# Loading the first chunks in pairs, with the first weight slices among them

## The chip, the cores and the metric

The kernel runs on one core of a Trainium2 chip. The metric is the device time of one launch in microseconds (us); lower is better. The time is 1.7 to 2.2 us longer than the span of the trace, which runs from the first to the last instruction.

The engines are called as in the profile: PE is TensorE (the matmuls), PEld its weight loads, DVE is VectorE, ACT is ScalarE, POOL is GpSimd, and SP is the engine that issues the data moves. "L565" is a line of the kernel.

## The reference, cut to what matters

```python
B, H, S, D = 4, 8, 768, 64              # q, k, v: float32
for t in range(S):                       # attention with a decaying state
    state = gamma[h] * state + outer(k[:, :, t], v[:, :, t])
    y[:, :, t] = (q[:, :, t] @ state) / sqrt(D)
x = y.transpose(0, 2, 1, 3).reshape(B * S, H * D)      # 3072 x 512
h = maximum(x @ w_in, 0.0)                             # 512 -> 2048
out = (h * h) @ w_out                                  # 2048 -> 512
```

A token's 64 numbers of one head lie together in memory, 256 bytes, and the next token of the same head follows. Two tokens of one head are therefore 512 bytes in one piece.

## The kernel before: the parts that matter

The 3072 tokens are 24 chunks of 128. For each chunk, q, k and v are loaded, cast to bf16, q and k are transposed ("turned") by PE or by the data queue, and a "visit" of PE computes scores, values and the state. DVE writes the result, scaled, to the tile `xt`. Then the first feed-forward matmuls (F1, L565) multiply `xt` by `w_in`, and the second ones (F2, L608) by `w_out`. F1 works on blocks of one to four chunks, and an F1 matmul has as many columns as the block has tokens.

```python
BLOCKS = [1, 1, 1, 1, 1, 1, 2, 2, 2, 4, 4, 4]     # chunks per F1 block
ORDER = (                                          # loads: i = slice of w_in, o = slice of w_out
    "k0 q0 q1 v0 k1 q2 v1 k2 v2 v3 k3 q3 i0 i1 q4 o0 i2 i3 k4 o1 v4 o2 o3 v5 v6 q5 k5 q6 v7 q7 k6 k7")
# ... (cut)
ld = {x: sb(f"{x}n", [P, NLD, H * D], FP32) for x in "qkv"}       # load tiles, after smaller tables
# ... (cut)
def prepare(m):                                    # one chunk: rows of 64 floats, 256 bytes
    for x in "kqv":
        t = ld[x][:, slot, :]
        # issued by SP (cut)
        q_.dma_start(t.rearrange("s (h d) -> s h d", h=H),
                     src[x][b, :, i * C : (i + 1) * C, :].rearrange("h s d -> s h d"))
    # ... casts of k and q on any of DVE, ACT, POOL; v times a table on DVE (cut)
# ... F2 of the last chunk is made in two half rows; prio decides their order (cut)
prio=(q4 + F2LAG) * 8 + 2 * j + 1 + part * 0.5
```

The order on each engine is not written by hand. A planner, run at build time, lays every operation in time by a model of the engines, the loads and the instruction fetches, and emits the instructions in that order. The planner also puts filler matmuls on PE while it waits at the start.

## Time and profile before

| | before |
|---|---|
| median of 3 runs | 216.29 us (215.98 to 216.98) |
| span of the profiled run | 214.5 us |
| first F1 matmul starts | 21.93 us |
| PE full and at full clock from | 26.3 us |
| last matmul ends | 210.4 us |

First the page of the profiled run: the span in 40 equal slices of 5.4 us. A digit is the busy share in tenths, PEclk is the granted clock of PE in tenths, and GB/s is what the data engines moved.

```profile
span 214.5 us, 6317 instructions
...
PE   6664899999999999999999999999999999999992
...
PEclk9965599999999999999999999999999999999999
...
GB/s 144 219 220 320 351 346 352 344 225 257 224 222 174 193 209 205 193 179 206 212 243 213 165 219 210 208 212 185 155 58 52 3 71 27 3 49 49 33 112 53
```

PE is full from the sixth slice to the end, so it bounds the kernel from there. The first five slices are different: PE is 40 to 90% busy, its clock falls to a half, and the loads move only about 220 GB/s in slices 2 and 3, against about 350 later. The same in the windows view; the columns are named by its first line, and the last two are the share of the 16 data engines and GB/s. The share adds up the times of all packets, and it is above 1 in places (1.34 at 5 to 11 us).

```profile
core 0: us, PE busy (x) PEld busy (x) DVE busy (x) ACT busy (x) POOL busy (x), PEclk, DMA share, GB/s
5.00:11.00 6.00, 4.20 (x80) 2.21 (x78) 2.99 (x6) 1.90 (x3) 2.45 (x4) 1.00 1.34 220
18.00:26.30 8.30, 6.84 (x136) 5.75 (x136) 5.55 (x12) 3.54 (x6) 2.73 (x4) 0.50 1.08 369
26.30:210.50 184.20, 183.37 (x2448) 108.83 (x2440) 100.68 (x205) 76.26 (x129) 30.78 (x47) 1.00 0.80 170
```

What PE waits for at first is in the chain of work that ended last, in order of time (start, duration, what):

```profile
13.32 7.64 DMA wst<-in_moe_w_in_dram
...
21.01 0.88 POOL w_in L345
...
21.93 3.59 PE fps L565 x32
```

Twelve loads of q, k and v are issued one behind the other until 13.3 us. Only then is the first slice of `w_in` issued, which takes 7.64 us to land and 0.88 to cast. The first 32 F1 matmuls then run at half clock.

The issue list gives the median time from issue to landing, and the waits of the data queue show what the end of the program waits for (total, times, longest, in us). The last view is of the loads and stores in the stretch from 210.5 to 214.5 us, in 40 slices of 0.1 us.

```profile
kn<-in_k_dram SPq DMA_DIRECT2D x24, 256.0 KB, 5.5
...
wst<-in_moe_w_in_dram SPq DMA_DIRECT2D x4, 1024.0 KB, 9.8
```

```profile
SPq L686 <- DMA out_dram<-osb: 2.1, 1, 2.1
```

### The profile page before, as it was taken

The numbers are of one execution on the slowest core, as the hardware profiler recorded it, in microseconds if no ns is written. First come the engines' busy times: TensorE is split into PE (matmuls) and PEld (weight loads), VectorE is DVE, ScalarE is ACT, GpSimd is POOL, SyncE is SP. The second block draws the span as 40 slices with busy tenths as digits, with TensorE's granted clock in tenths as the row PEclk, the third lists the DMA queues.
The fourth block names the chain that finished last, engine by engine and source line by source line (L and its number), as shares of the span: only waits on it lengthen the run. The fifth ranks groups of instructions, "written<-read, shape, count | busy, mean of one in ns | idle before, by whom it ended". The sixth has DMA issues, their size and how long they took to land.

```text
span 214.5 us, 6317 instructions
## 1 busy us (share of the span) xinstructions
PE 200.8 (94%) x2764; PEld 119.8 (56%) x2764; DVE 115.4 (54%) x249; ACT 87.5 (41%) x145; POOL 39.9 (19%) x68
## 2 busy tenths in 40 slices
PE   6664899999999999999999999999999999999992
PEld 2343899675467787666654444454444444444461
DVE  1567778775148699666745674656654433322100
ACT  8223368643234264433321644223534325534211
POOL 5413322314321222122231213132100000000000
PEclk9965599999999999999999999999999999999999
DMA  7999999999999999989999999999811010011021
GB/s 144 219 220 320 351 346 352 344 225 257 224 222 174 193 209 205 193 179 206 212 243 213 165 219 210 208 212 185 155 58 52 3 71 27 3 49 49 33 112 53
DMA packets 99627, 38.15 MB, mean 178 GB/s; under 512 B 92304, under 2 KB 92560, under 8 KB 99600
## 3 DMA queue, kind: packets, MB, share of 16 engines
q1 hardware_dynamic: 99600, 37.76, 81.8%
q8 instruction: 21, 0.34, 0.7%
q14 instruction: 6, 0.05, 0.1%
HBM read 27.26 MB, written 6.29 MB: 156 GB/s over the span
## 4 chain that ended last, share of the span: by engine, by line
PE 83%; DMA 6%; SPq 6%; ACT 1%; issue 1%; POOL 0%; DVE 0%; ACTq 0%
PE fps L608 38%; PE fps L565 38%; SPq L355 6%; DMA wst<-in_moe_w_in_dram 4%; DMA qkT<-kqs 3%; PE yy L425 2%; PE yy L440 2%; PE sc L451 1%; PE sc L462 1%; ACT qkT L387 0%; PE fps L408 0%; POOL w_in L345 0%; ACT osb L616 0%; PE yy L381 0%; DVE xt L527 0%
## 5 line engine op out<-in xcount | busy, mean ns | idle before, releaser
L565 PE MATMUL fps<-xt,w_in 128*128 128x128 bf16 (+2 forms) x768 | 94.0, 276 | 0.7 <-POOL w_in L345 0.6
L608 PE MATMUL fps<-w_out,h 128*128 128x512 bf16 (+1 forms) x400 | 92.2, 371 | 0.0
L570 ACT ACTIVATE h<-fps 128x512 bf16<-128x512 f32 x96 | 57.3, 597 | 75.2 <-PE fps L565 75.2
L565 PEld LDWEIGHTS <-w_in 128*128 128x128 bf16 x768 | 60.6, 100 | 29.1 <-POOL w_in L345 0.8
L575 DVE TENSOR_TENSOR h<-h 128x512 bf16<-128x512 bf16 x96 | 44.2, 469 | 48.3 <-ACT h L570 48.1
L608 PEld LDWEIGHTS <-h 128*128 128x128 bf16 x400 | 37.5, 98 | 36.8
L616 ACT ACTIVATE osb<-fps 128x512 f32<-128x512 f32 (+1 forms) x25 | 14.5, 580 | 31.5 <-PE fps L608 30.4
L345 POOL CAST kqs<-kn 128x512 bf16<-128x512 f32 x24 | 15.9, 664 | 56.3 <-DMA kn<-in_k_dram 46.8
L527 DVE TENSOR_TENSOR xt<-yy,yf 128x512 bf16<-128x512 f32 x24 | 16.5, 687 | 16.2 <-PE yy L440 13.3
L345 POOL CAST kqs<-qn 128x512 bf16<-128x512 f32 x24 | 15.7, 654 | 37.5 <-DMA qn<-in_q_dram 37.5
L366 DVE TENSOR_TENSOR vs<-vn,vf 128x512 bf16<-128x512 f32 x24 | 17.7, 740 | 7.2 <-DMA vn<-in_v_dram 7.2
L505 DVE TENSOR_TENSOR pt<-sc,cmask 128x512 bf16<-128x512 f32 x24 | 16.3, 680 | 4.8 <-PE sc L462 4.8
L518 DVE TENSOR_TENSOR state<-sc,state 128x256 bf16<-128x256 f32 x40 | 16.7, 418 | 0.7
L440 PE MATMUL yy<-qkT,state 64*64 64x64 bf16 x352 | 12.3, 203 | 0.5
L408 PE MATMUL fps<-ident,kqs 128*128 128x128 bf16 x48 | 5.6, 249 | 4.6 <-POOL kqs L345 4.6
L425 PEld LDWEIGHTS <-vs 64*64 64x64 bf16 x384 | 5.3, 112 | 7.6 <-issue 7.4
L462 PE MATMUL sc<-vs,kqs 64*64 64x64 bf16 x352 | 7.9, 198 | 1.1 <-DVE vs L366 1.1
L451 PE MATMUL sc<-qkT 64*64 64x64 bf16 x384 | 7.7, 198 | 1.2 <-ACT qkT L341 0.7
L440 PEld LDWEIGHTS <-state 64*64 64x64 bf16 x352 | 7.7, 112 | 1.2 <-PE yy L440 1.2
L341 ACT ACTIVATE qkT<-fps 128x512 bf16<-128x512 bf16 x6 | 3.6, 597 | 11.3 <-PE fps L408 11.3
L408 PEld LDWEIGHTS <-kqs 128*128 128x128 bf16 x48 | 3.4, 108 | 8.2 <-POOL kqs L345 7.7
L425 PE MATMUL yy<-pt,vs 64*64 64x64 bf16 x384 | 8.0, 203 | 0.0
(32 smaller groups left out, 53.5 us busy)
## 6 DMA issues: line engine op xcount, KB each, us to landing
kn<-in_k_dram SPq DMA_DIRECT2D x24, 256.0 KB, 5.5
qn<-in_q_dram SPq DMA_DIRECT2D x24, 256.0 KB, 5.3
vn<-in_v_dram SPq DMA_DIRECT2D x24, 256.0 KB, 5.2
out_dram<-osb SPq DMA_DIRECT2D x23, 256.0 KB, 2.8
wst<-in_moe_w_in_dram SPq DMA_DIRECT2D x4, 1024.0 KB, 9.8
wst<-in_moe_w_out_dram SPq DMA_DIRECT2D x4, 1024.0 KB, 10.6
qkT<-kqs SPq DMA_TRANSPOSE x16, 4.6
out_dram<-osb SPq DMA_DIRECT2D x2, 128.0 KB, 2.2
```

What stands on the lines that cost most here:

```text
L345: nc.gpsimd.tensor_copy(o, t)
L366: lambda: nc.vector.tensor_tensor(out=o[:], in0=t.rearrange("s (h d) -> s h d", h=H), in1=vf[:, i, :, None].to_broadcast([P, H, D]), op=AL ...
L425: nc.tensor.matmul(yy[L * c : L * c + L, sub, p * L : p * L + L], lhsT=vs[r, 4 * a + j, :], rhs=pt[r, a, j, :], start=(p == 0), stop=True, ...
L440: nc.tensor.matmul(yy[L * c : L * c + L, sub, p * L : p * L + L], lhsT=st[r, j, :], rhs=qkT[r, 1, j, sub * L : sub * L + L], start=False, ...
L505: lambda: nc.vector.tensor_tensor(out=pt[:], in0=sc[:, :, 0:256].rearrange("s g (p t) -> s g p t", p=NJ), in1=cmask[:, None, None, :].to_b ...
L518: f = lambda cc=cc, j1=j1, j0=j0: nc.vector.tensor_tensor(out=sts[j1][:], in0=cc, in1=sts[j0][:], op=ALU.add)
L527: lambda: nc.vector.tensor_tensor(out=xt[:, :, u * C : u * C + C].rearrange("s p (g t) -> s g p t", g=2), in0=yy[:, :, 0:256].rearrange("s ...
L565: nc.tensor.matmul(ps[:, u * n : u * n + n], lhsT=w_in_bf[j][:, cb, c * P : (c + 1) * P], rhs=xt[:, cb, cols], start=(cb == 0), stop=(cb = ...
L570: nc.scalar.activation(h2[:, f0 : f0 + per, cols], ps[:].rearrange("p (u n) -> p u n", u=per), AF.Relu)
L575: nc.vector.tensor_mul(hv, hv, hv)
L608: nc.tensor.matmul(ps[:, 0:w], lhsT=h2[:, fb, u * C : u * C + C], rhs=w_out_bf[j][:, c, ns], start=(fb == 0), stop=(fb == NFB - 1))
L616: lambda o1=o1, slot=slot, ns=ns, w=w: nc.scalar.activation(osbs[slot][:, ns], fps[o1["op"]["bank_index"]][:, 0:w], AF.Copy),
```

## The change

Its intent is to bring the first weights earlier by making the early loads faster. Chunks 0 and 1, and chunks 2 and 3, are loaded as pairs: row s of the tile holds tokens 2s and 2s+1, so that each piece is 512 bytes. The tokens are then in the wrong rows. For k and v, PE puts them in order by matmuls with a 0/1 matrix ("placing"), and ACT copies the result out of the accumulator. For q and k, even and odd tokens are turned apart and written interleaved. The first slice of `w_in` goes between the pairs. Chunks 8 and 9, which the data queue turned, are turned by PE. Block sizes begin with 2. Forty tiny matmuls of one column stand at the head of PE's program. The last two half rows are made one after the other. The planner's model got finer constants too.

```diff
-BLOCKS = [1, 1, 1, 1, 1, 1, 2, 2, 2, 4, 4, 4]
+BLOCKS = [2, 1, 1, 1, 1, 2, 4, 2, 2, 4, 4]
-WARM = 20.0
-FILL = 0.8
-PACE = 8
+WARM = 14.0
+FILL = 0.215
+WARMING = 5.5
+PACE = 6
-NPE = 6
-NTD = 8
+NPE = 7
+NTD = 10
+PRE = 40
+NPAIR = 2
... (planner constants and engines for casts cut)
 ORDER = (
-    "k0 q0 q1 v0 k1 q2 v1 k2 v2 v3 k3 q3 i0 i1 q4 o0 i2 i3 k4 o1 v4 o2 o3 v5 v6 q5 k5 q6 v7 q7 k6 k7"
+    "k0 v0 q0 k2 v2 i0 q2 i1 q4 i2 o0 o1 k4 i3 k5 v4 q5 o2 q6 v5 v6 o3 q7 k6 k7 v7"
 )
... (cut)
+    def together(n):
+        b, i = where(2 * n)
... (cut)
+                   lambda x=x: nc.sync.dma_start(
+                       rows_(x).rearrange("s (h n) -> s h n", h=H),
+                       src[x][b, :, i * C : (i + 2) * C, :].rearrange("h (s g) d -> s h (g d)", g=2)),
... (casts, turning of even and odd tokens cut)
+                    for g in range(2):
+                        nc.tensor.matmul(ps[:], lhsT=perm[r, g, :], rhs=twin[name][r, g, :], start=(g == 0), stop=(g == 1))
... (cut)
-                                prio=(q4 + F2LAG) * 8 + 2 * j + 1 + part * 0.5, lat=0.2,
+                                prio=(q4 + F2LAG) * 8 + 2 * j + 1 + part * 9, lat=0.2,
... (cut)
+            one = nc.const_aps.tensor(1.0, [P, 1], BF16)
+            for _ in range(PRE):
+                nc.tensor.matmul(fps[NBANK - 1][0:1, 0:1], lhsT=one, rhs=one, start=True, stop=True)
```

More of the change, by code (lines that the diff above doesn't have):

```diff
@@ L26 @@
     DMA_LATENCY = 1.9
+    GEN_LATENCY = 1.65
     LAND = 1.25
@@ L82, in schedule @@
                     pool[e].add(o["i"])
-        bank_free = [0.0] * (nbanks - 1) + [WARM]
+        if "PE" in eng_free:
+            eng_free["PE"] = 0.06 * PRE
+        bank_free = [0.0] * (nbanks - 1) + [WARM + 1]
         bank_of = {}
         open_groups = set()
-        pipe = 0.0
+        pipe = made = 0.0
+        late = []
         outstanding = {e: [] for e in eng_free}
         done = 0
-        issued, edge, next_fetched, history, crossed = 0, self.BLOCK0, 3.0, [], 0.0
+        issued, edge, next_fetched, history, crossed = 2 * PRE, self.BLOCK0, 3.0, [], 0.0
         while done < n:
@@ L116, in schedule @@
             if move:
-                cost, n_desc, hold = dur
+                gen, cost, n_desc, hold = dur
                 out_ = outstanding[eng]
@@ L132, in schedule @@
                 eng_free[eng] = t + hold
-                pipe = max(pipe, t + self.DMA_LATENCY) + cost
-                end[i] = pipe + self.LAND
-                out_.append((pipe, n_desc))
+                if n_desc:
+                    made = max(made, t + self.GEN_LATENCY) + gen
+                    ready = made + 0.15
+                else:
+                    ready = t + hold + 0.5
+                pipe = max(max(pipe, t + self.DMA_LATENCY) + cost, ready)
+                late = [y for y in (max(max(y, t + self.DMA_LATENCY) + cost, ready) for y in late) if y > pipe + 0.05]
+                end[i] = max([pipe] + late) + self.LAND
+                out_.append((max([pipe] + late), n_desc))
                 dur = hold
@@ L139, in schedule @@
                     o["fill"] = 0
-                    if t < WARM:
-                        o["fill"] = int(max(0.0, t - max(eng_free[eng], 1.5) - 0.3) * FILL / 0.427)
+                    if WARM - WARMING < t < WARM + 1:
+                        o["fill"] = int(max(0.0, t - max(eng_free[eng], WARM - WARMING) - 0.1) / FILL)
                     issued += 2 * o["fill"]
+                    before = issued
                     todo, per = 2 * o["count"], dur / max(1, 2 * o["count"])
@@ L156, in schedule @@
                     history.append((issued, t + dur))
+                    if any(before < x <= issued for x in range(self.BLOCK0 - self.AHEAD, issued + 1, self.BLOCK)):
+                        late.append(max(pipe, t + 0.4) + 1.27)
                     o["dur"] = dur
@@ L174, in schedule @@
         return sorted(range(n), key=lambda i: (start[i], i))
-SMALL = (1.20, 65, 0.6)
-TURN = (1.10, 16, 2.4)
-WIDE = (2.85, 33, 0.6)
-STORE = (0.80, 9, 0.6)
-BLOCKS = [1, 1, 1, 1, 1, 1, 2, 2, 2, 4, 4, 4]
+SMALL = (1.20, 0.93, 65, 0.6)
+TWIN = (1.20, 1.75, 65, 0.6)
+TURN = (0.60, 1.10, 16, 2.4)
+WIDE = (0.60, 2.80, 33, 0.6)
+STORE = (0.30, 0.80, 9, 0.6)
+BLOCKS = [2, 1, 1, 1, 1, 2, 4, 2, 2, 4, 4]
 SPLIT = 6
 AHEAD = 4
-WARM = 20.0
-FILL = 0.8
-PACE = 8
+WARM = 14.0
+FILL = 0.215
+WARMING = 5.5
+PACE = 6
 LEAD = 2
-NPE = 6
-NTD = 8
-QACT = 0
+NPE = 7
+NTD = 10
+PRE = 40
+CVT = {'DVE': 0.69, 'POOL': 1.1}
+TCAST = {'DVE': 0.43, 'ACT': 0.63, 'POOL': 0.78}
+TEVAC = {'ACT': 0.6, 'DVE': 0.62}
+MEVAC = {'ACT': 0.6}
+NPAIR = 2
 F2LAG = 3.0
@@ L244 @@
         assert 512 % (n * C) == 0 and x // 4 == (x + n - 1) // 4
-    NLD, NBF, NQT, NXT, NH2, NWS, NOSB, NST = 4, 5, 5, 4, 3, 4, 3, 6
+    NLD, NBF, NQT, NXT, NH2, NWS, NOSB, NST = 4, 6, 6, 4, 3, 4, 3, 6
     NBANK = 4
@@ L260 @@
     vf = sb("vf", [P, NCH, H], FP32)
-    pos_i = sb("pos_i", [P, S], I32)
     yf = sb("yf", [P, NJ, S], FP32)
@@ L266 @@
     bf["v"] = [sb(f"vs{j}", [P, H, D], BF16) for j in range(NBF)]
-    qkts = [sb(f"qkT{j}", [P, 2, NJ, P], BF16) for j in range(NQT)]
+    qkt_all = sb("qkT", [P, NQT, 2, NJ, P], BF16)
+    qkts = [qkt_all[:, j] for j in range(NQT)]
+    perm = sb("perm", [P, 2, P], BF16)
+    ex2_i = sb("ex2_i", [P, NCH // 2, 2], I32)
+    ex2_f = sb("ex2_f", [P, NCH // 2, 2, H], FP32)
+    vf2 = sb("vf2", [P, NCH // 2, 2, H], FP32)
     pts = [sb(f"pt{j}", [P, 2, NJ, L], BF16) for j in range(2)]
@@ L271 @@
     h2s = [sb(f"h2{j}", [P, NFB, 512], BF16) for j in range(NH2)]
+    twins = [{x: h2s[NH2 - 1][:, 6 * j + 2 * "qkv".index(x) : 6 * j + 2 * "qkv".index(x) + 2, :] for x in "qkv"}
+             for j in range(2)]
+    pos_i = h2s[NH2 - 1][:, 12:15, :].rearrange("p a n -> p (a n)").bitcast(I32)
     w_in_bf = [sb(f"w_in{j}", [P, NCB, 512], BF16) for j in range(4)]
@@ L315, in halflogs, with placing @@
                 nc.vector.memset(lnt[L * c : L * c + L, p : p + 1], float(np.log(gammas[4 * a + 2 * b + c])))
+    def placing():
+        nc.gpsimd.memset(perm[:], 0.0)
+        for half in range(2):
+            r = slice(L * half, L * half + L)
+            nc.gpsimd.affine_select(out=perm[r], in_=perm[r], compare_op=ALU.not_equal,
+                                    fill=1.0, base=0, pattern=[[-1, 2], [1, P]], channel_multiplier=-2)
     pl.add("iota", "POOL", 0.2, (), ("ex_i",),
@@ L322 @@
     pl.add("cmask", "POOL", 0.9, (), ("cmask",), mask, prio=-96)
+    pl.add("perm", "POOL", 1.2, (), ("perm",), placing, prio=-95.5)
+    pl.add("iota3", "POOL", 0.2, (), ("ex2_i",),
+           lambda: nc.gpsimd.iota(ex2_i[:], pattern=[[2 * C, NCH // 2], [1, 2]], base=0, channel_multiplier=2), prio=-98.5)
     pl.add("lng", "DVE", 0.4, (), ("lng",), logs, prio=-99)
@@ L332 @@
            lambda: nc.vector.tensor_scalar_mul(vf[:], vf[:], scale), prio=-99)
+    pl.add("ex2_f", "DVE", 0.2, ("ex2_i", "lng"), ("ex2_f",),
+           lambda: nc.vector.tensor_tensor(
+               out=ex2_f[:], in0=ex2_i[:, :, :, None].to_broadcast([P, NCH // 2, 2, H]),
+               in1=lng[:, None, None, :].to_broadcast([P, NCH // 2, 2, H]), op=ALU.mult), prio=-99)
+    pl.add("vf20", "ACT", 0.3, ("ex2_f",), ("vf2",),
+           lambda: nc.scalar.activation(vf2[:], ex2_f[:], AF.Exp, scale=-1.0), prio=-99.5)
+    pl.add("vf2", "DVE", 0.2, ("vf2",), ("vf2",),
+           lambda: nc.vector.tensor_scalar_mul(vf2[:], vf2[:], scale), prio=-99)
     def ytable():
@@ L336, in ytable @@
             nc.scalar.activation(yf[:, p, :], pos_i[:], AF.Exp, scale=lnt[:, p : p + 1])
-    pl.add("yf", "ACT", 3.4, ("pos_i", "lnt"), ("yf",), ytable, prio=-98)
+    yf_made = pl.add("yf", "ACT", 3.4, ("pos_i", "lnt"), ("yf",), ytable, prio=-98)
     def copy_on(eng, o, t):
@@ L345, in copy_on, with turn_fn, place @@
             nc.gpsimd.tensor_copy(o, t)
+    twin_users = [yf_made]
+    def together(n):
+        b, i = where(2 * n)
+        m, s0, w, twin = 2 * n, (2 * n) % NLD, n % 2, twins[n % 2]
+        rows_ = lambda x: ld[x][:, s0 : s0 + 2, :].rearrange("s u n -> s (u n)")
+        held = lambda x: (f"ld{x}{s0}", f"ld{x}{s0 + 1}")
+        for x in "kqv":
+            pl.add(f"ld{x}{m}", "SP", TWIN, (), held(x),
+                   lambda x=x: nc.sync.dma_start(
+                       rows_(x).rearrange("s (h n) -> s h n", h=H),
+                       src[x][b, :, i * C : (i + 2) * C, :].rearrange("h (s g) d -> s h (g d)", g=2)),
+                   prio=dma_prio[(x, m)])
+        for g in range(2):
+            for x in "kq":
+                o = twin[x][:, g, :].rearrange("s (j a d) -> s a j d", a=2, j=NJ)
+                t = rows_(x).rearrange("s (a j g d) -> s a j g d", a=2, j=NJ, g=2)[:, :, :, g, :]
+                pl.add(f"c{x}{m}.{g}", TCAST, 0, held(x), (f"twin{x}{w}.{g}",),
+                       lambda on, t=t, o=o: copy_on(on, o, t), prio=urgency(m))
+            t = rows_("v").rearrange("s (h g d) -> s h g d", h=H, g=2)[:, :, g, :]
+            pl.add(f"cv{m}.{g}", CVT, 0, held("v") + ("vf2",), (f"twinv{w}.{g}",),
+                   lambda on, t=t, g=g: (nc.vector if on == "DVE" else nc.gpsimd).tensor_tensor(
+                       out=twin["v"][:, g, :].rearrange("s (h d) -> s h d", h=H), in0=t,
+                       in1=vf2[:, i // 2, g, :, None].to_broadcast([P, H, D]), op=ALU.mult),
+                   prio=urgency(m))
+        q0 = m % NQT
+        for g in range(2):
+            for x, name in enumerate("kq"):
+                o1 = {}
+                def turn_fn(x=x, name=name, g=g, o1=o1):
+                    ps = fps[o1["op"]["bank_index"]].bitcast(BF16)
+                    for j in range(NJ):
+                        nc.tensor.transpose(ps[:, j * P : j * P + P], twin[name][:, g, j * P : j * P + P], ident[:])
+                i0 = pl.add(f"T{name}{m}.{g}", "PE", 0.26, (f"twin{name}{w}.{g}", "ident"), (f"gT{name}{m}{g}",), turn_fn,
+                            prio=-200 + m, lat=0.2, count=4, bank=("open", ("T", m, x, g), False))
+                twin_users.append(i0)
+                o1["op"] = pl.ops[i0]
+                pl.add(f"E{name}{m}.{g}", TEVAC, 0, (f"gT{name}{m}{g}",),
+                       (f"qkT{q0}.{name}{g}", f"qkT{q0 + 1}.{name}{g}"),
+                       lambda on, x=x, g=g, o1=o1: copy_on(
+                           on, qkt_all[:, q0 : q0 + 2, x].rearrange("p c j (t g) -> p c j t g", g=2)[:, :, :, :, g],
+                           fps[o1["op"]["bank_index"]].bitcast(BF16)[:, 0:512].rearrange("p (j c t) -> p c j t", j=NJ, c=2)),
+                       prio=urgency(m), lat=0.05, bank=("close", ("T", m, x, g)))
+        for c in range(2):
+            r = slice(L * c, L * c + L)
+            for name in "kv":
+                o1 = {}
+                def place(name=name, r=r, o1=o1):
+                    ps = fps[o1["op"]["bank_index"]]
+                    for g in range(2):
+                        nc.tensor.matmul(ps[:], lhsT=perm[r, g, :], rhs=twin[name][r, g, :], start=(g == 0), stop=(g == 1))
+                i0 = pl.add(f"N{name}{m + c}", "PE", 0.45, (f"twin{name}{w}.0", f"twin{name}{w}.1", "perm"), (f"gN{name}{m + c}",),
+                            place, prio=-190 + m + c, lat=0.2, count=2, bank=("open", ("N", m + c, name), False))
+                twin_users.append(i0)
+                o1["op"] = pl.ops[i0]
+                o = bf[name][(m + c) % NBF]
+                o = o.rearrange("s j a d -> s (j a d)") if name == "k" else o.rearrange("s h d -> s (h d)")
+                pl.add(f"M{name}{m + c}", MEVAC, 0, (f"gN{name}{m + c}",), (f"bf{name}{(m + c) % NBF}",),
+                       lambda on, o=o, o1=o1: copy_on(on, o, fps[o1["op"]["bank_index"]][:]),
+                       prio=urgency(m + c), lat=0.05, bank=("close", ("N", m + c, name)))
@@ L348, in prepare @@
     def prepare(m):
+        if m < 2 * NPAIR:
+            if m % 2 == 0:
+                together(m // 2)
+            return
         b, i = where(m)
@@ L352, in prepare @@
             t = ld[x][:, slot, :]
-            side = x == "q" and m < QACT
-            pl.add(f"ld{x}{m}", "ACT" if side else "SP", SMALL, (), (f"ld{x}{slot}",),
-                   lambda x=x, t=t, q_=nc.scalar if side else nc.sync: q_.dma_start(
+            pl.add(f"ld{x}{m}", "SP", SMALL, (), (f"ld{x}{slot}",),
+                   lambda x=x, t=t: nc.sync.dma_start(
                        t.rearrange("s (h d) -> s h d", h=H),
                        src[x][b, :, i * C : (i + 1) * C, :].rearrange("h s d -> s h d")),
-                   prio=dma_prio[(x, m)] - 200 * side)
+                   prio=dma_prio[(x, m)])
         for x in "kq":
@@ L371, in qkeys @@
     def qkeys(m):
-        return [f"qkT{m % NQT}.{x}" for x in "kq"]
+        return [f"qkT{m % NQT}.{x}{g}" for x in "kq" for g in range(2)]
     def flips(m):
@@ L394, in transpose @@
         qkT, t = qkts[m % NQT], kq[m % NBF]
-        if NPE <= m < NTD:
+        if m < 2 * NPAIR or NPE <= m < NTD:
             return
@@ L411, in transpose @@
             o1["op"] = pl.ops[i0]
-            pl.add(f"E{name}{m}", EVAC, 0, (f"gT{name}{m}",), (qkeys(m)[x],),
+            pl.add(f"E{name}{m}", EVAC, 0, (f"gT{name}{m}",), qkeys(m)[2 * x : 2 * x + 2],
                    lambda on, x=x, o1=o1: copy_on(on, qkT[:, x].rearrange("p j t -> p (j t)"),
@@ L582, in ffn1 @@
             pl.add(f"R{blk}.{f0}", "ACT", 0.6, (f"g{grp}",), hk, relu,
-                   prio=blk0[blk] + f0 / 16 * nb, bank=("close", grp))
+                   prio=blk0[blk] + f0 / 16 * nb, bank=("close", grp),
+                   after=twin_users if g == NH2 - 1 else ())
             pl.add(f"Q{blk}.{f0}", "DVE", 0.43, hk, hk, square, prio=blk0[blk] + f0 / 16 * nb + 2)
@@ L656 @@
                 for _ in range(o.get("fill", 0)):
-                    nc.tensor.matmul(fps[NBANK - 1][:], lhsT=ident[:],
-                                     rhs=ident[:, None, :].to_broadcast([P, 4, P]), start=True, stop=True)
+                    nc.tensor.matmul(fps[NBANK - 1][:, 0 : 2 * P], lhsT=ident[:],
+                                     rhs=ident[:, None, :].to_broadcast([P, 2, P]), start=True, stop=True)
                 o["fn"](o["on"]) if o["flex"] else o["fn"]()
```

## The prediction

> **What bounds it now.** The windows view shows TensorE (PE) busy 183.35 of the 184.18 us between 26.32 and 210.5 us, at full granted clock. PE binds from there on. The start is bound by loads: in the chain of waits the load queue issues until 13.3 us, the first w_in slice takes 7.64 us to land, its cast 0.9, and the first FFN matmul starts at 21.93. The granted clock is 0.50 from about 13 to 26 us, so the first 32 FFN matmuls take 3.59 us instead of 1.79.
>
> **Why the load is slow.** In the windows of 1 us the twelve q, k, v loads before the weights move 214 to 230 GB/s (4.5 to 16 us; nearly all packets under 512 B), the weight loads after them 390 to 414. [...] Pairing makes the rows 512 B. My estimate is about 300 GB/s, 1.75 us for 512 KB against 2.4 for two loads now.
>
> **Change, step by step.**
> - Removed: the first w_in slice now follows five pair loads (about 9 us of data, estimate) instead of twelve single ones (14.4). It should land near 14.5 to 15.5, and the first FFN matmul start at about 15.7: 6.2 us earlier.
> - Added, mostly in PE time that waits anyway: eight placing groups (two 512-column matmuls each, about 0.43 to 0.85 us), their ACT evacuations (0.6 each). Two more chunks turned by PE instead of the DMA queue cost about 0.9 us net in the saturated part.
> - Block sizes are neutral: 16 FFN matmuls of 128 columns take 0.89, 8 of 256 columns 0.87.
> - Not regained: after the change only two chunks are ready at the first slice (1.8 us of work), and the second slice lands about 4.5 us after the first, since a pair load lies between. I expect 1.5 to 2 us idle at about 17.5 to 20 us, and perhaps a second cold phase[...] (warm at 6 to 12.5 us, cold after 12.5 at 40 to 75% busy).
> - Tail: the last two half-row groups one after the other instead of interleaved hide one 0.38 us evacuation.
> - The 40 tiny matmuls lie before any data: worth nothing by themselves.
>
> **Sum.** Work left at 26.32 us before: 183.3. For a start at 15.7 add first FFN group 1.8, visits 2 and 3 about 2, late turns 0.6, extra turns 0.75: 188.4. Plus 2 idle, 0.9 of scattered gaps, 0.5 to 1 of cold clock: last matmul at about 207.7 instead of 210.4. With the tail, about 3.2 us of 216.3 saved.
>
> **Predicted: 213.0 us**, 8 in 10 between 209.8 and 215.8. Chances: faster by over 2% 0.31, within 2% 0.64, slower 0.05.
>
> **What would show it.** GB/s in the first 11 us near 300, not 220; first FFN matmul at 15 to 16.5; a PE gap and perhaps a clock of 0.5 at 17 to 22; PE full from 25 us.
>
> **What would make it wrong.** Pair loads at 350 GB/s or more and a warm clock throughout (209 to 211). Or ACT, which alone evacuates the placed rows, delaying the first visits; the fourth w_in slice, moved behind two w_out slices, starving PE near 30 us; the early four-chunk block waiting for chunk 11 near 80 us (then 215 or more).

The 300 GB/s is the author's estimate; it lies between the two rates measured in the trace of the kernel before (214 to 230 and 390 to 414), and how the rate goes with the length of the rows had not been shown. The 0.5 to 1 us of cold clock is an estimate too, after the clock of 0.50 in the same trace.

## More of the kernel before

The kernel before had a median of 216.41 us in the batch of the first comparison and 215.77, 215.73 and 216.12 us in the three batches of experiments.

```profile
GB/s 0 0 0 0 0 0 0 10 236 338 358 266 113 215 348 317 266 72 82 0 0 0 31 20 20 10 0 0 0 0 0 0 0 0 0 0 0 0 0 0
...
q14 instruction: 1, 0.01, 0.6%
```

The last stores are nearly done at 212.4 us, but a few packets trail at 10 to 31 GB/s until 213.1, and an instruction fetch lies in the same stretch. The program waits 2.1 us for this.

## The result, and the profile after

| | before | after |
|---|---|---|
| median, 4 runs each | 216.41 us (215.98 to 216.98) | 213.19 us (212.94 to 213.53) |
| ratio | 1 | 0.9851, 95% interval 0.9821 to 0.988 |
| span of the profiled run | 214.5 us | 211.8 us |
| first F1 matmul starts | 21.93 us | 19.51 us |
| PE full and at full clock from | 26.3 us | 21.35 us |
| last matmul ends | 210.4 us | 208.65 us |
| from there to the end of the span | 4.1 us | 3.1 us |

A ratio is the mean time of one kernel's fast runs over that of the other's fast runs of the same rounds, so it is not quite the ratio of the medians quoted. The kernel is 1.5% faster, inside the band of 2% that counts as the same. A second batch, given below as a control, measured 213.76 us and 0.9922, so there the kernel gained 0.8%.

The page of the kernel after:

```profile
span 211.8 us, 6380 instructions
...
PE   2898999999999999999999999999999999999994
...
PEclk9999999999999999999999999999999999999999
...
GB/s 167 290 344 343 348 352 239 302 300 183 268 217 210 184 219 190 258 206 233 173 238 211 203 227 220 237 165 76 0 53 50 3 50 50 3 51 50 0 102 99
```

GB/s in the second slice went from 219 to 290. PE is 80% busy or more from the second slice, but much of that is placing and filler. The clock row now reads 9 from the start, and here it misleads. The trace records changes of the clock, and the first recorded one is at 21.36 us; before it the row shows full clock because nothing was recorded. The instructions tell otherwise. The F1 matmuls at 19.51 us need 1.91 us for eight of 256 columns; at 21.73 us the trace has sixteen in 1.92 us. PE ran at half speed until about 21.36 us. That was not fixed by the program: t2 below has the same instructions up to its end, and its trace has full clock from 11.6 to 18.4 us (a mean of 0.94 over the first 26.32 us).

The windows view of the kernel after, with the same columns as before:

```profile
5.00:11.00 6.00, 4.87 (x27) 2.32 (x28) 3.06 (x6) 3.97 (x8) 3.81 (x4) 1.00 1.21 290
...
21.35:208.70 187.35, 186.62 (x2569) 111.00 (x2568) 103.78 (x216) 79.11 (x134) 31.44 (x47) 1.00 0.80 168
```

The second line accounts for PE's gain. PE is saturated 4.95 us earlier (26.3 less 21.35), but it has 3.25 us more left to do (186.62 less 183.37), and its gaps in the stretch fell from 0.83 to 0.73. That is 4.95 - 3.25 + 0.1 = 1.8 us, and the last matmul ends 210.41 - 208.65 = 1.8 us earlier.

The timeline around the first slice of `w_in` (start, duration, engine, and in brackets the idle time before and who ended it) shows why F1 does not start right after it:

```profile
14.92 0.61 POOL L392 CAST w_in<-wst 128x512 bf16<-128x512 f32 x1 [0.70 <-DMA wst<-in_moe_w_in_dram]
...
16.68 0.42 DVE L390 CAST w_in<-wst 128x512 bf16<-128x512 f32 x1
...
18.00 0.63 ACT L388 ACTIVATE h<-qn 128x512 bf16<-128x512 f32 x1 [0.54 <-DMA qn<-in_q_dram]
...
18.24 0.69 DVE L642 TENSOR_TENSOR xt<-yy,yf 128x512 bf16<-128x512 f32 x1 [0.35 <-PE yy L555]
...
18.68 1.03 PE L430 MATMUL fps<-ident,h 128*128 128x128 bf16 x8 [0.50 <-ACT h L388]
19.51 0.63 PE L680 MATMUL fps<-xt,w_in 128*128 128x256 bf16 x2
```

The slice has landed at 14.9 us and its last quarter is cast at 17.10. But the first block now has two chunks, and the result of chunk 1 is written only at 18.93. In PE's order the turning of q of chunks 2 and 3 comes first as well. Its load was issued behind the slice, and it arrives at 18.0.

Last, the same views of the loads and of the end of the program. The third fence is the stretch from 208 to 211.8 us in 40 slices.

```profile
wst<-in_moe_w_in_dram SPq DMA_DIRECT2D x4, 1024.0 KB, 10.0
...
kn<-in_k_dram SPq DMA_DIRECT2D x2, 512.0 KB, 7.1
```

```profile
SPq L805 <- DMA out_dram<-osb: 1.2, 1, 1.2
```

```profile
GB/s 22 22 162 323 366 345 184 22 0 0 0 0 0 0 0 0 0 0 0 0 162 345 345 345 162 22 0 0 0 0 0 0 0 0 0 0 0 0 0 0
```

The two half rows go out one after the other, nothing trails, and the wait is 1.2 us instead of 2.1. So the difference of the spans, 2.7 us, has two parts: 1.8 us from the start, and about 1 us from the end (4.1 less 3.1 us). The times of the two profiled runs, 216.62 and 213.53 us, differ by 3.1; the remaining 0.4 us lies outside the spans, and no view shows it.

### The profile page after: what moved, and what is told of

It reads as the page before. It is cut to its first block, busy times and chain, and to the rows that moved or that the text cites. A ratio compares the mean times of both kernels' runs of the same rounds, so it can differ in the third digit from the quotient of the medians.

```text
span 211.8 us, 6380 instructions
## 1 busy us (share of the span) xinstructions
PE 202.2 (95%) x2788; PEld 119.9 (57%) x2788; DVE 114.4 (54%) x253; ACT 94.7 (45%) x157; POOL 42.4 (20%) x70
## 4 chain that ended last, share of the span: by engine, by line
PE 74%; DMA 18%; SPq 4%; ACT 1%; DVE 1%; POOL 1%; issue 0%
PE fps L724 36%; PE fps L680 31%; DMA wst<-in_moe_w_out_dram 13%; DMA wst<-in_moe_w_in_dram 5%; SPq L406 3%; PE yy L540 2%; PE yy L555 1%; PE sc L577 1%; PE sc L566 1%; ACT qkT L502 1%; SPq L656 1%; DVE xt L642 1%; PE yy L496 1%; POOL w_out L392 0%; ACT osb L732 0%
## 5 line engine op out<-in xcount | busy, mean ns | idle before, releaser
L680 PE MATMUL fps<-xt,w_in 128*128 128x256 bf16 (+2 forms) x704 | 93.8, 284 | 0.1
L680 PEld LDWEIGHTS <-w_in 128*128 128x128 bf16 x704 | 58.6, 98 | 31.0 <-issue 0.7
L690 DVE TENSOR_TENSOR h<-h 128x512 bf16<-128x512 bf16 x96 | 42.2, 448 | 51.8 <-ACT h L685 51.3
L732 ACT ACTIVATE osb<-fps 128x512 f32<-128x512 f32 (+1 forms) x25 | 14.5, 580 | 32.7 <-PE fps L724 32.4
L392 POOL CAST kqs<-kn 128x512 bf16<-128x512 f32 x19 | 12.4, 654 | 55.2 <-DMA kn<-in_k_dram 42.2
L392 POOL CAST kqs<-qn 128x512 bf16<-128x512 f32 x20 | 13.5, 675 | 16.5 <-DMA qn<-in_q_dram 16.5
L481 DVE TENSOR_TENSOR vs<-vn,vf 128x512 bf16<-128x512 f32 x20 | 13.9, 697 | 2.5 <-DMA vn<-in_v_dram 2.5
L430 PE MATMUL fps<-ident,h 128*128 128x128 bf16 x32 | 4.3, 308 | 4.1 <-DVE h L390 3.5
L388 ACT ACTIVATE qkT<-fps 128x512 bf16<-128x512 bf16 x7 | 4.8, 698 | 5.9 <-PE fps L523 3.5
L390 DVE COPY qkT<-fps 128x512 bf16<-128x512 bf16 x7 | 3.9, 556 | 4.7 <-PE fps L523 1.9
```

What stands on the lines that cost most here:

```text
L392: nc.gpsimd.tensor_copy(o, t)
L481: lambda: nc.vector.tensor_tensor(out=o[:], in0=t.rearrange("s (h d) -> s h d", h=H), in1=vf[:, i, :, None].to_broadcast([P, H, D]), op=AL ...
L680: nc.tensor.matmul(ps[:, u * n : u * n + n], lhsT=w_in_bf[j][:, cb, c * P : (c + 1) * P], rhs=xt[:, cb, cols], start=(cb == 0), stop=(cb = ...
L690: nc.vector.tensor_mul(hv, hv, hv)
L732: lambda o1=o1, slot=slot, ns=ns, w=w: nc.scalar.activation(osbs[slot][:, ns], fps[o1["op"]["bank_index"]][:, 0:w], AF.Copy),
```

## The experiments

All outputs are right. Each batch ran on one chip with its own runs of the kernel before (11 runs each). Short names are used below: t1 and t2 swap the order of the last half rows, t3 and t4 add instructions on ACT, w1 starts the filler earlier, l1 loads the weights last, n1 has no pairs, k1 and k2 have single blocks, p0 has no tiny matmuls, a1 has moved load tiles, and c0 is the kernel after again, the control. The control ran in one of the three batches only, with k2, p0 and t3, so elsewhere a comparison with the kernel after goes from batch to batch.

In t1, t2, t3, t4 and a1 the built programs have the same instructions in the same order as the kernel that they start from, except for the edit. In w1, l1, n1, k1, k2 and p0 the planner also reordered other work, on PE and on the engines that cast, so these runs compare whole plans.

### The end: which of two causes gained 1 us

Theory: the new order of the half rows hides work. Rival: something else moved the instruction fetch away from the last store. Two kernels swap only the order.

```diff
# t1: the kernel before
-                                prio=(q4 + F2LAG) * 8 + 2 * j + 1 + part * 0.5, lat=0.2,
+                                prio=(q4 + F2LAG) * 8 + 2 * j + 1 + part * 9, lat=0.2,
# t2: the kernel after, the other way round (9 -> 0.5)
```

> The kernel before, with only the new order of the last two half rows (part * 9 for part * 0.5). The prediction said 0.4 us for the tail. Theory (from the two traces: last matmul 210.41 to end 214.5 before, 208.65 to 211.8 after, so 0.94 us): the time falls by 0.9 us, to about 215.4. If 0.4 was right, 216.0. If nothing, 216.4.

> The changed kernel with the old interleaved order of the last two half rows. Theory: the tail is worth 0.9 us there too, so 214.1 against 213.2. Rival (0.4 us as predicted): 213.6.

The kernel before with the new order took 216.11 us, ratio 1.0017 (0.9986 to 1.0048). The kernel after with the old order took 213.74 us, ratio 0.9908 (0.9879 to 0.9937), as the kernel after itself in the control (213.76, 0.9922). The order of the half rows has no effect that these runs resolve. It is t1 that speaks against a gain of 0.9 us, which would be a ratio of 0.996, outside its interval; t2 is compared with a control of another batch, and 0.9 us is less than batches differ. The wait for the last store in both, the new order in the kernel before first, the old order in the kernel after second:

```profile
SPq L686 <- DMA out_dram<-osb: 2.0, 1, 2.0
```

```profile
SPq L805 <- DMA out_dram<-osb: 1.2, 1, 1.2
```

The wait follows the kernel, not the order. Over all the traces the wait is 2.1 us in the kernel before, 2.0 in t1, and 1.2 in every other one. What differs is the fetch. In the kernel before and in t1 the view of the last few us lists an instruction fetch ("q14 instruction: 1" above), and in the kernel after it does not. In the packet records the fetches on q14 (8 KB each: 6 packets, 0.05 MB) follow ACT's progress, and the last one comes when ACT is at about its 192nd record. ACT has 194 records in the kernel before and 220 in the kernel after, so this fetch comes at 185.56 us instead of 212.31. That can be tried directly, by giving ACT in the kernel before twelve tiny instructions more. It took two attempts.

```diff
# t3: the kernel before
+    spare = sb("spare", [P, 1], FP32)          # after lng, lnt
+    # after each of the first 12 evacuations of F2 (cut):
+    nc.scalar.activation(spare[:, 0:1], lng[:, 0:1], AF.Copy)
# t4: the same twelve instructions, into a tile that exists
+    nc.scalar.activation(ex_f[:, 0, 0:1], lng[:, 0:1], AF.Copy)
```

> The kernel before with twelve more tiny ACT instructions (one after each of the first twelve output evacuations, result unused). Theory: in the traces an 8 KB instruction fetch follows ACT's 191st to 194th record; before, that is at 212.31 us, in the middle of the last store (1.77 us from first to last packet), after the change at 185.56 and the last store waits 1.2 us instead of 2.1. With twelve more instructions the fetch falls before 200 us and the end comes 0.9 us sooner with no other change: about 215.4 against 216.3, ratio 0.996. Rival: the shorter store comes from the new order of the last half rows or of the loads; then no gain, ratio 1.000.

> The kernel before with the same twelve tiny ACT instructions as t3, written to a tile that is already there, so that no tile moves. t3 gained 2.7 us, but its one new 4-byte tile also moved every later tile by 32 bytes: the load tiles began 480 bytes past a multiple of 512 before and at a multiple of 512 in t3, and its single loads ran at 250 GB/s for 218. Theory: the instruction fetch at the end is worth 0.9 us, the alignment the other 1.8: 214.8 here, ratio 0.996, loads at 218 GB/s. Rival 1: the fetch is all of it: 213.0. Rival 2: alignment is all of it: 215.7.

The first attempt took 213.04 us, ratio 0.9867 (0.984 to 0.9894). That is 2.7 us faster, three times what the wait could give, so it could not be the fetch alone. The new tile had moved all tiles behind it; the section on addresses follows that up. The second attempt, with no tile moved, took 215.84 us, ratio 0.9989 (0.9956 to 1.0022). Its waits of the data queue:

```profile
SPq L687 <- DMA out_dram<-osb: 1.2, 1, 1.2
```

The fetch now comes at 197.57 us, again at ACT's 191st record. So the trace confirms the theory: with the fetch away from the end the wait is 1.2 instead of 2.1 us, and the time from the last matmul to the end is 3.2 us instead of 4.1. The time does not confirm it: 0.9 us is 0.4%, and the interval holds both 1 and 0.996. The profiled run of t4 lost about as much before its end: its last matmul ended at 211.23 us instead of 210.41. The tail gain is shown in traces, not in times.

### Cold clock or order: why F1 started at 19.5 us

Theory A: PE would have been earlier if it were warm. Rival B: F1 waits in order behind work whose data come late. This kernel starts the filler earlier, so that PE warms up sooner.

```diff
-WARMING = 5.5
+WARMING = 13.0
```

> The changed kernel with about 16 more filling matmuls of 256 columns from 2 us on (WARMING 13 for 5.5). Theory cold PE: placing matmuls take 427 ns each start to start at half clock from 6 to 17 us and PE is full from 9 to 18 us, so a warm PE brings the first FFN matmul from 19.5 to 17 us or earlier and the time falls by 1 to 2 us. Rival chain: the first FFN matmul waits for the second chunk's row of casts, evacuations and visits on ACT, DVE and POOL, and the first w_in slice is cast only by 17.1; then the clock gives under 0.5 us, and the FFN matmul stays after 18.5.

PE did warm up, with full clock from 12.0 to 18.8 us, and it did not help:

```profile
18.90 1.03 PE L430 MATMUL fps<-ident,h 128*128 128x128 bf16 x8 [1.58 <-ACT h L388]
19.73 0.63 PE L680 MATMUL fps<-xt,w_in 128*128 128x256 bf16 x2
```

The faster PE simply waits 1.58 us, instead of 0.50, for the cast of the late q load, and F1 starts at 19.73. The clock was down again after the wait (the first eight F1 matmuls took 1.91 us, as in the kernel after), and the kernel took 214.82 us, ratio 0.9967 (0.9933 to 1.0). w1 also has another plan than the kernel after, but t2 does not, and its profiled run happened to have full clock from 11.6 to 18.4 us. PE waited for the same cast, and F1 started no earlier:

```profile
18.91 1.03 PE L430 MATMUL fps<-ident,h 128*128 128x128 bf16 x8 [1.81 <-ACT h L388]
19.73 1.91 PE L680 MATMUL fps<-xt,w_in 128*128 128x256 bf16 x8
```

Theory A falls and B holds.

If B holds, one might put all pairs before the weights. That was tried last:

```diff
-    "k0 v0 q0 k2 v2 i0 q2 i1 q4 i2 o0 o1 k4 i3 k5 v4 q5 o2 q6 v5 v6 o3 q7 k6 k7 v7"
+    "k0 v0 q0 k2 v2 q2 i0 i1 q4 o0 i2 i3 k4 o1 v4 o2 k5 q5 o3 q6 v5 v6 q7 k6 k7 v7"
```

> The changed kernel with all six pair loads before the first weight slice (pairs, but no slice among them). My reading of the trace: the first FFN matmuls at 19.5 us waited in PE's order behind the turning of q of chunks 2 and 3, whose load landed only at 18.0 because it lay behind the first slice. With q loaded first the slice lands about 1.7 us later (16.6), its FFN matmuls still start at about 18.5 to 19.5, so the time is within 0.7 us of the changed kernel: 213 to 214.5. If the early slice matters as the change intends: 1.5 us or more slower.

It took 216.1 us, ratio 1.0014 (0.9976 to 1.0052), worse than expected. F1 started at 19.96, only 0.45 us later, but new gaps came elsewhere:

```profile
18.54 0.23 PE L566 MATMUL sc<-qkT 64*64 64x64 bf16 x5 [0.87 <-issue]
...
47.52 0.31 PE L577 MATMUL sc<-vs,kqs 64*64 64x64 bf16 x8 [1.19 <-DVE vs L481]
```

The second gap is a wait for a v load whose place I had also changed. The first one ends 1.5 us after an instruction fetch (see the block sizes below), and right before F1 PE waited 1.07 us for a result of DVE (`xt`). So this run mixes several things, and how much of the loss belongs to the place of the first slice stays open.

### What the pairs are worth

```diff
-PRE = 40
+PRE = 72
-NPAIR = 2
+NPAIR = 0
 ORDER = (
-    "k0 v0 q0 k2 v2 i0 q2 i1 q4 i2 ... (same after this)
+    "k0 v0 q0 k1 v1 q1 k2 v2 i0 k3 v3 q2 q3 i1 q4 i2 ... (same after this)
```

> The changed kernel without pairs (NPAIR 0): single loads, no placing matmuls, the first w_in slice still among the loads (after chunk 2), 72 tiny matmuls as the place of fetches that suits this order. If the pairs carry the gain: first slice lands 3 us later (218 GB/s for 290) and the time is 2 to 3 us longer than with pairs, 215.5 to 216.5. If the early place of the weight slices alone carries it: 213 to 214.

With single loads, and the plan that the planner makes for them, the kernel took 218.26 us, ratio 1.0107 (1.0073 to 1.0141), slower than the kernel before. PE stood before F1:

```profile
18.29 0.80 PE L680 MATMUL fps<-xt,w_in 128*128 128x256 bf16 x3 [2.27 <-DVE xt L642]
```

Its F1 starts earlier than in the kernel after (18.29 against 19.51), but not as early as PE could have: the slice landed at 16.46 us, 1.5 us later than in the kernel after although only eight single loads stand before it instead of five pairs (ten), its last cast ended at 17.64, and the result of chunk 1 came behind two of these casts on DVE, at 18.24. PE's gaps that end after 18 us (those over 0.12 us, here and below) sum up to 5.3 us, against 0.74 in the kernel after. Of the 5.3 us, 1.83 are waits for casts of `w_out`. Its last matmul ends 4.4 us later, about the difference of the gaps. So the other parts of the change, as planned here, do not pay without the pairs. That the pairs carry all of the gain is not shown: the tiny matmuls went to 72 here, to keep the fetches near their place, and a changed plan alone can cost 3 us (p0 below). The pairs in the kernel before, with nothing else, were not run, nor were the turning of chunks 8 and 9 and the planner's new constants tried alone.

### Block sizes, called neutral in the prediction

```diff
-BLOCKS = [2, 1, 1, 1, 1, 2, 4, 2, 2, 4, 4]
+BLOCKS = [1, 1, 1, 1, 1, 1, 2, 4, 2, 2, 4, 4]     # k1; k2 also has PRE = 112 for 40
```

> The changed kernel with the first block of two chunks cut into two blocks of one. Theory: the first FFN matmuls then need only chunk 0 (its xt was ready at 16.2 us) and start at about 17.2, when the cast of the first w_in slice ends; that is 2 us earlier, but at half clock and with the same total, so 0.3 to 1 us faster. Rival: the start is not the limit but the arrival of slices (the second one at 20.8 us): then within 0.3 us of the changed kernel.

> As k1 (first block cut in two), but with 112 tiny matmuls for 40. k1 was 217.0, with issue gaps of 0.99 and 1.49 us on PE at 25 and 31 us. Theory fetch: the cut block has 128 more instructions early, the gaps come from where the fetches fall, and shifting them removes most of it: 213.5 to 215. Rival: the smaller block itself is the loss: 216.5 or more again.

The first took 217.01 us, ratio 1.0064 (1.0031 to 1.0097). That is 3 us or more slower than the kernel after (1.0064 against 0.9851 and 0.9922). Its profiled run was its slowest, 218.34 us. F1 started at 16.94 us, 2.6 us earlier, and the gain was lost in gaps. In the two largest PE waited for nothing that the profile shows ("issue"):

```profile
25.97 0.28 PE L566 MATMUL sc<-qkT 64*64 64x64 bf16 x9 [0.99 <-issue]
...
32.72 0.95 PE L680 MATMUL fps<-xt,w_in 128*128 128x128 bf16 x14 [1.49 <-issue]
```

Each of these gaps ends 1.3 to 1.4 us after the last packet of an instruction fetch for PE (fetches of 23.30 to 24.60 and 30.12 to 31.42 us), in stretches in which the loads keep the data engines busy (share 1.09 at 20 to 26 and at 26 to 32 us). The kernel after has fetches that end at 24.1 and 30.6 us too, and no such gap follows them. A block of one chunk needs 64 F1 matmuls of 128 columns, where a block of two needs the same 64 with 256 columns, for twice the tokens. In the kernel before, 16 matmuls of 128 columns take 0.89 us and 8 of 256 columns 0.87, so PE uses up its instructions about twice as fast just then. My theory was that the place of the fetches is to blame, and that k2, which shifts them by 72 more tiny matmuls, would be back at 213.5 to 215 us. It took 216.86 us, ratio 1.0056 (1.0022 to 1.0089), against 213.76 for the control in the same batch. The forecast was wrong, but the gaps had not simply moved:

```profile
18.19 1.15 PE L680 MATMUL fps<-xt,w_in 128*128 128x128 bf16 x16 [1.83 <-POOL w_in L392]
...
23.38 0.40 PE L523 MATMUL fps<-ident,kqs 128*128 128x128 bf16 x4 [1.14 <-POOL kqs L392]
...
30.14 0.25 PE L540 MATMUL yy<-pt,vs 64*64 64x64 bf16 x7 [1.15 <-issue]
```

Two of the three largest are waits for casts on POOL, which the new plan brought. Of the "issue" gaps over 0.2 us one is left, of 1.15 us, where k1 had four with 3.6 us in all. So k2 does not test the theory cleanly. The traces of all runs speak for it: of the gaps over 0.2 us that end after 18 us, the eleven "issue" ones (in k1, k2, p0, l1, w1 and a1) all end 1.3 to 1.7 us after the last packet of a fetch for PE, while most fetches have no such gap behind them. What is shown is that single blocks, with the plan that goes with them, cost about 3 us here; that fetches cause the "issue" gaps is argued from this coincidence in time, not shown.

### The forty tiny matmuls

```diff
-PRE = 40
+PRE = 0
```

> The changed kernel without the 40 tiny matmuls (PRE 0). My prediction said that they are worth nothing. Theory now: [...] the 80 tiny instructions shift these fetches to where PE is not waiting; without them PE stands idle with nothing to wait for (issue gaps of 0.5 us or more between 20 and 60 us, 2 us in all) and the time is 1.5 to 2.5 us longer, about 215.2. Rival: same as the changed kernel within 0.4 us.

What the page of the kernel after shows is 22 fetches on q8 with 0.36 MB, so 16 KB each, which took 0.8% of the span of 16 engines, so about 1.2 us each.

> The changed kernel as it is, as a control on the chip of these runs: ratio near 0.985 of before, as measured at first.

The control is the kernel after unchanged. One of its runs, the profiled one, took 409.73 us and is not used (its 512-column F2 matmuls took 676 ns in the mean instead of 379; why is open). Five have a median of 213.76 us, and gave 0.9922 (0.9902 to 0.9943). Without the tiny matmuls the kernel took 216.92 us, ratio 1.0078 (1.0038 to 1.0118), 3.2 us more. So, with the plan that goes with them, they are worth as much as the change itself. The trace of the kernel without them has 4.44 us of gaps on PE after 18 us, against 0.74. The largest is

```profile
22.57 0.61 PE L523 MATMUL fps<-ident,kqs 128*128 128x128 bf16 x4 [2.06 <-POOL kqs L392]
```

PE waits here for the load of q of chunk 4, because the planner has put its turning one F1 group earlier than in the kernel after. The planner counts the tiny matmuls as instructions, so that without them it expects fetches elsewhere and orders PE's work otherwise. Of the gaps over 0.2 us in this trace, 2.6 us are waits for casts and 1.2 us "issue" gaps after fetches, so waits for data are the larger part there. How the 3.2 us divide stays open: the test, the same order with the forty matmuls left out only when the instructions are emitted, was not run.

### Addresses of the load tiles

The 2.7 us of t3 needed a cause. In the addresses that the build gives, the tiles for q, k and v begin 480 bytes past a multiple of 512 in both kernels, because of the small tables before them. The one 4-byte tile of t3 takes 32 bytes and puts them, and every tile behind them, on a multiple of 512. Its windows and issues:

```profile
5.00:11.00 6.00, 4.48 (x99) 2.39 (x101) 3.78 (x8) 2.50 (x4) 2.35 (x4) 1.00 1.09 248
```

```profile
kn<-in_k_dram SPq DMA_DIRECT2D x24, 256.0 KB, 4.1
```

The single loads move 248 GB/s instead of 220, the data engines' share falls from 1.34 to 1.09, and a load lands in 4.1 us instead of 5.5. t4, with the same instructions and the old addresses, loads at 218 GB/s. The direct test is the kernel after with one unused tile, and no instruction changed:

```diff
     lnt = sb("lnt", [P, NJ], FP32)
+    spare = sb("spare", [P, 1], FP32)
```

> The changed kernel with one unused 4-byte tile, so that the load tiles begin at a multiple of 512 instead of 480 past one; no instruction differs. Theory alignment: the pair loads run faster than 290 GB/s (330 or more), slices land 1 us or more earlier and the time falls by 1 to 2.5 us, to 211 to 212.5. Rival: 512-byte rows are not slowed by the offset as 256-byte rows were: the same pair rate and 213.5 to 214.

It took 210.81 us (210.44 to 211.5), ratio 0.9769 (0.9737 to 0.98). It is the fastest of all, 2.3% faster than the kernel before and 0.8 to 1.5% faster than the kernel after by ratio (0.9769 against 0.9851 and 0.9922, both from other batches; their intervals and this one do not overlap). Its windows, its first F1 matmul and its pair loads:

```profile
5.00:11.00 6.00, 5.74 (x37) 2.72 (x41) 4.05 (x6) 4.49 (x8) 3.11 (x5) 1.00 1.14 357
```

```profile
17.53 1.03 PE L681 MATMUL fps<-xt,w_in 128*128 128x256 bf16 x8 [0.25 <-DVE xt L643]
```

```profile
kn<-in_k_dram SPq DMA_DIRECT2D x2, 512.0 KB, 5.0
```

The early stretch moves 357 GB/s instead of 290 (it holds some of the first slice too; in windows of 2 us from 4 to 10 us, where the pairs are, the rate is 344 to 348, against 291 to 301), and a pair lands in 5.0 us instead of 7.1. F1 starts 2 us earlier and at full speed, eight matmuls in 1.03 us (the recorded clock is full from 11.5 us on). The gaps on PE after 18 us sum up to 0.28 us, and the last matmul ends at 205.84 instead of 208.65.

Why the destination in the core's memory matters no run shows; what they show is 218 against 248 GB/s for single loads and 290 against 348 for pairs. Which multiple is needed they do not show either, since no other address was tried. The tile also moved everything behind it, the casts' outputs and tiles of the matmuls among them. By the build, the staging tiles of the weights lie 416 bytes past a multiple of 512 in a1 and on one in t3, while q, k and v lie on one in both. The rate of the loads is what the traces show to have changed.

## Why the prediction was right or wrong

The time was right: 213.0 us predicted, 213.19 and 213.76 measured. But it was right by errors that cancel each other, so the close hit is luck, and this is the more useful finding. The saving was predicted as 3.2 us and measured as 3.2 in the first comparison and 2.0 in the control.

**Right.** The first slice was to land at 14.5 to 15.5 us and its cast began at 14.92. The pair loads were to move about 300 GB/s and moved 290. The parts of the added work were about right: the visits of chunks 2 and 3 took 1.9 us of PE in the saturated part, counted from start to start (2 predicted), the additional turning 0.82, counted likewise (0.75 predicted). PE was cold at 17 to 21.4 us as thought possible, with the difference that the trace shows no warm phase before that (eight F1 matmuls of 256 columns took 1.91 us at 19.51, and eight turning matmuls 1.03 us both at 12.14 and at 18.68). In the kernel before the recorded warm phase lasted 6.827 us (from 5.83 to 12.65) and the cold one 13.653 (to 26.31); what sets these lengths, and what makes the clock fall, no run shows.

**Wrong: "the first FFN matmul start at about 15.7".** It started at 19.51, later by 3.8 us. Three terms were left out, and the timeline gives them. The slice's cast was done at 17.10, not by 15.7, because its four quarters were shared by POOL, ACT and DVE and the last one came behind two other operations of DVE: 1.4 us. The first block has two chunks and chunk 1 was ready at 18.93: 1.83 us. The turning of q of chunks 2 and 3 stood before F1 on PE, and its load behind the first slice: 0.58 us. I had cost the parts and left out the order of PE.

**Wrong, in the other direction: "1.5 to 2 us idle" and "0.9 of scattered gaps".** After 18 us, PE's gaps sum up to 0.74 us. Because F1 began late, the second slice was there when it was needed. "PE full from 25 us" came at 21.35. Of the 2.7 us that PE's end was to gain it gained 1.8.

**Wrong: "Tail: ... hide one 0.38 us evacuation".** The swap of the order was worth nothing that could be resolved (t1, t2). The end did gain about 1 us, in the traces by an instruction fetch that ACT's 26 additional records moved away from the last store (from 212.31 to 185.56 us; the wait fell from 2.1 to 1.2). This made up for about half of the 0.9 us that PE's part fell short of.

**Wrong: "The 40 tiny matmuls ... worth nothing by themselves".** Taking them away, and planning anew, costs 3.2 us. The prediction looked at their own time and not at their place in the program and in the planner's count.

**Wrong: "Block sizes are neutral".** The busy time of F1 is nearly equal, as predicted (95.6 us in k1, 93.8 in the kernel after), but single blocks cost 3 us or more, in gaps. How they arise is open in part: the kernel's plan changes with the blocks.

**Incomplete: rows under 512 bytes as the reason for the slow loads.** Pairing did raise the rate, from 220 to 290 GB/s, and to 348 with aligned tiles. But single loads of 256 bytes also rose to 248 when the tile was moved by 32 bytes. Of the distance from 220 to 348, which is 128 GB/s, the address alone gives 28 on single loads and 58 on pairs, so between a quarter and a half of it. The prediction put it all down to the length of the rows. And 512-byte rows on aligned tiles still stayed under the weight loads, which moved 389 to 414 GB/s in the kernel before at 18 to 22 us.

## What to carry to other kernels

Look at the addresses of load tiles first: one unused 4-byte tile, which put the load tiles on a multiple of 512 bytes, gained the kernel before 2.7 us (with twelve ACT instructions that alone gave nothing resolvable) and the changed one 0.8 to 1.5%, about what the whole change had gained. When loads are moved forward, follow PE's own order to the first useful matmul: what stands before it, and when does the last input of its block come, is what set the start here, not the landing of the weights alone (the slice landed at 14.9 us, and F1 started at 19.51). A piece of work that costs nothing in busy time, such as smaller matmuls or forty tiny ones, can still move the time by 3 us where a planner depends on the count (3.2 us in p0, about 3 in k1 and k2), so it is worth a run of its own.
